# The first chunk's output product in seven half-size products, with the weights' sums scheduled sooner and their signs turned on ScalarE

## The chip, the cores and the metric

The kernel runs on one core of a Trainium2 chip. The metric is the device time of one execution in microseconds (us); the time before is the median of three runs. A profile of one execution gives the work of each engine: TensorE (PE, matmuls), VectorE (DVE), ScalarE (ACT), GpSimd (POOL), the DMA queues and the queue of SyncE (SP).

## The reference

For each of 4 batches, `q`, `k` and `v` are 6016 x 256. `q` and `k` are normalised over the 6016 rows of each column, a 256 x 256 matrix of scores is formed from them, and its softmax `a` is applied to `v`. The result, 24064 rows of 256, goes through a gated network: with `w_gate` and `w_val` of 256 x 1536 and `w_out` of 1536 x 256,

```
s = kn.transpose(0, 2, 1) @ qn / tau        # kn, qn: k, q over their column norms
a = softmax(s);  x = v @ a
out = (sigmoid(x @ w_gate) * (x @ w_val)) @ w_out
```

## The kernel before

**Folded weights.** Because `x = v @ a`, the kernel multiplies `a` into `w_gate` and `w_val` once for each batch (tiles `gh_G`, `gh_H`, function `gh`). The network then takes `v` itself, transposed into `vT`.

**Chunks and slots.** A batch is 47 tiles of 128 rows, in 12 chunks of up to 4 tiles (512 rows). A chunk has 12 *slots*, one for each 128 of the 1536 hidden columns. In a slot `glu` makes `ps_gate` (two matmuls of 512 columns, then a tanh on ScalarE, L662, into `g_sb`) and `ps_val` (two matmuls), and VectorE joins both into one slice of `hT` (L665). `ps_gate` and `ps_val` have two buffers each, so the gate of a slot needs the tanh of two slots before to be done. Slot numbers here run on over the chunks of a batch: slots 12 to 23 are those of the second chunk.

**The output product lies one chunk behind.** While chunk n runs through its 12 slots, the product of chunk n - 1's `hT` with `w_out` is done in twelve portions, one in each slot between gate and val (`run_work`, called through `mid`). Two forms of it exist:

- *plain* (`single`): for each of 4 row tiles, 12 matmuls of 256 columns that add up over the hidden columns; then one copy on ScalarE (L775). The first chunk of batch 0 alone is done so (`plain`).
- *seven products* (`product`): rows and columns are halved, and four half-size blocks are formed from seven products in place of eight, as in Strassen's scheme in Winograd's form. One round is for one pair of row tiles (p is 0 or 1), and each product is six matmuls of 128 columns. It needs sums and differences of blocks of `hT`, made on VectorE by `a_sum` (L691, L693, L695, tile `sums`, in two rounds for a chunk: `OWN_SLOTS` 7, 9, 11 of its own slots, `NEXT_SLOTS` 0, 2, 4 of the next chunk's), and of blocks of `w_out`, made once on GpSimd by `sum_w_out` (L232, tile `w_sums`, five sums in three pieces each). Sum 4 is also multiplied by -1 (L234). The order of the products is in `ORDER`: y1 of both pairs first (sum 1), then x1 (sum 0), z1 (sum 3), x2 and y2 (blocks of `w_out` itself), z2 (sum 2) and v2 (sum 4). `part` and `whole` put the seven results together: two copies on ScalarE for a pair, and four additions on GpSimd.

**The order of the work** is the order of the program: the scheduler is off (`manual_schedule`), each engine runs its own instructions in the order written, and waits only for what an instruction needs. `side_work` hangs further work on slots with `at(slot, function, ...)`; it is issued at the end of its slot. For batch 0: copying `w_out` to bf16 (`copy_w_out`, slot 8, L225), loads of the next batch's `q` and `k` (`load_qk`, L150) and of `v` (L162), the scores of the next batch (plain, from slot 14), the squares for its norms on ScalarE (L258), and the sums of `w_out` in slots 11, 13, 15, 17 and 19. The loads of `q`, `k`, `v` and of the weights are issued from GpSimd's queue; `w_out` is the last of the weights (L220, three pieces of 512 KB).

Of the kernel before, what the change touches and what calls it, by code (L numbers as in the profile page):

```python
# [12 lines left out]
ACT = mybir.ActivationFunctionType  # L13
ALU = mybir.AluOpType
# [37 lines left out]
OWN_SLOTS = {7: 0, 9: 1, 11: 2}  # L52
# [3 lines left out]
def kernel(  # L56
# [20 lines left out]
    nc = tc.nc  # L77
# [10 lines left out]
    FC = DFF // P  # L88
# [41 lines left out]
    def mm(out, lhsT, rhs, start, stop, **kw):  # L130
        nc.tensor.matmul(out, lhsT=lhsT, rhs=rhs, start=start, stop=stop, **kw)  # L131
# [34 lines left out]
    t0, nt = groups0[0]  # L166
# [39 lines left out]
    for f0, nf in pieces:  # L206
        if f0 + nf == DFF:
            load_v(0, 1)
        for w, src in enumerate((moe_w_gate, moe_w_val)):
            nc.gpsimd.dma_start(  # L210
                out=w_sb[w][f0 // FG][:, :, ds(f0 % FG, nf)],
                in_=src.rearrange("(t p) f -> p t f", p=P)[:, :, ds(f0, nf)],
# [5 lines left out]
    for n in range(FC // TPC):  # L218
        w_f32[n] = f32pool.tile([P, TPC, C], FP32, tag="f32", name="w_f32")
        nc.gpsimd.dma_start(  # L220
            out=w_f32[n], in_=moe_w_out.rearrange("(t p) c -> p t c", p=P)[:, n * TPC : (n + 1) * TPC, :]
# [5 lines left out]
    def sum_w_out(m, n):  # L227
        (k0, c0), op, (k1, c1) = B_SUMS[m]
        w = w_f32[n]
        out = w_sums[:, m, n * 2 : (n + 1) * 2, :]  # L230
        in0, in1 = w[:, k0::2, ds(c0 * P, P)], w[:, k1::2, ds(c1 * P, P)]
        nc.gpsimd.tensor_tensor(out=out, in0=in0, in1=in1, op=op)  # L232
        if m == 4:
            nc.gpsimd.tensor_scalar(out=out, in0=out, scalar1=-1.0, scalar2=None, op0=ALU.mult)  # L234


    st = {}
# [460 lines left out]
    stores = []  # L698

    def out_tile(b, ci):  # L700
        if (b, ci) not in ffn:
            ffn[b, ci] = opool.tile([P, TPC, C], FP32, tag="osb", name="out_sb")
        return ffn[b, ci]

    def out_work(b, ci):

        nt = groups[ci][1]
        half = nt // 2
        hT = hts[b, ci]
        work = []  # L710
        states = [{} for _ in range(half)]
        singles = {}
        plain = (b, ci) == (0, 0)

        def product(p, name, i):
            state = states[p]
            region, a, w = PRODUCTS[name]
            first = name == "y1" and i == 0
            if first:
                state["ps"] = pso.tile([P, CH], FP32, tag="o", name="ps_o")  # L720
            g, j = divmod(i, FC // 4)
            if isinstance(a, tuple):
                lhsT = hT[:, 2 * i + a[1], ds((a[0] * half + p) * P, P)]
            else:
                lhsT = sums[b, ci, g][:, a, j, ds(p * P, P)]
            rhs = w_out_sb[:, 2 * i + w[0], ds(w[1] * P, P)] if isinstance(w, tuple) else w_sums[:, w, i, :]
            mm(
                state["ps"][:, ds(region * P, P)],
                lhsT,
                rhs,  # L730
                start=first,
                stop=(i == FC // 2 - 1),
                skip_group_check=True,
            )
            if i == FC // 2 - 1:
                if name == "z1":
                    part(p)
                elif name == "v2":
                    whole(p)

        def part(p):

            m = states[p]["m"] = mpool.tile([P, 3, P], FP32, tag="m", name="m_sb")
            nc.scalar.copy(m, states[p]["ps"][:, : 3 * P].rearrange("p (n c) -> p n c", c=P))  # L744
            nc.gpsimd.tensor_tensor(out=m[:, 1, :], in0=m[:, 1, :], in1=m[:, 2, :], op=ALU.add)  # L745
            nc.gpsimd.tensor_tensor(out=m[:, 2, :], in0=m[:, 1, :], in1=m[:, 0, :], op=ALU.add)  # L746

        def whole(p):

            o = out_tile(b, ci)  # L750
            nc.scalar.copy(  # L751
                o[:, p : p + half + 1 : half, :],
                states[p]["ps"].rearrange("p (t c) -> p t c", c=C),
            )
            blocks = o.rearrange("p t (h c) -> p (t h) c", c=P)
            c00, c11 = 2 * p, 2 * (half + p) + 1
            ends = blocks[:, c00 : c11 + 1 : c11 - c00, :]
            mids = blocks[:, c00 + 1 : c11 : max(1, c11 - c00 - 2), :]
            last = (b, ci) == (B - 1, NCH - 2)
            add = nc.gpsimd.tensor_tensor  # L760
            add(out=ends, in0=ends, in1=states[p]["m"][:, 1:3, :], op=ALU.add)  # L761
            add(out=ends, in0=ends, in1=mids, op=ALU.subtract)  # L762
            if last:
                t0 = groups[ci][0]
                nc.sync.dma_start(out=out_rows[b][:, t0 + p : t0 + nt : half, :], in_=o[:, p:nt:half, :])
            elif p == half - 1:
                stores.append((b, ci))

        def single(s, f):
            if f == 0:  # L770
                singles[s] = pso.tile([P, CH], FP32, tag="o", name="ps_o")
            ps = singles[s]
            mm(ps[:, :C], hT[:, f, ds(s * P, P)], w_out_sb[:, f, :], f == 0, f == FC - 1)
            if f == FC - 1:
                nc.scalar.copy(out_tile(b, ci)[:, s, :], ps[:, :C])  # L775
                if plain and s == nt - 1:
                    stores.append((b, ci))

        if plain:
            return [(2, single, t, f) for t in range(nt) for f in range(FC)]  # L780
        for p, name in LAST_ORDER if (b, ci) == (B - 1, NCH - 2) else ORDER:
            if p < half:
                for i in range(FC // 2):
                    work.append((1, product, p, name, i))
                if nt % 2 and name == "z1":
                    for f in range(FC):
                        work.append((2, single, nt - 1, f))
        return work

    def run_work(work, share):  # L790

        upto = sum(w[0] for w in work) * share
        done = 0
        while work and done < upto:
            cost, fn, *args = work.pop(0)
            fn(*args)
            done += cost

    def store():
        while stores:  # L800
            b, ci = stores.pop(0)
            t0, nt = groups[ci]
            nc.sync.dma_start(out=out_rows[b][:, t0 : t0 + nt, :], in_=ffn.pop((b, ci))[:, :nt, :])
# [111 lines left out]
    def side_work(b):  # L915
# [4 lines left out]
        def at(slot, fn, *a):  # L920
            side.setdefault(divmod(slot, FC), []).append((fn, a))

        for ci in range(NCH):
            nb, nci = (b, ci + 1) if ci + 1 < NCH else (b + 1, 0)
            lb, lci = (b, ci + 2) if ci + 2 < NCH else (b + 1, ci + 2 - NCH)
            if nb < B:
                at(ci * FC + 2, transpose_v, nb, nci)
            if lb < B:
                at(ci * FC + (10 if (b, ci) == (0, 0) else 0), load_v, lb, lci)
            if (b, ci) == (0, 0):  # L930
                for i in range(FC // TPC):
                    at(8, copy_w_out, i)
                for n, m in enumerate((1, 0, 3, 2, 4)):
                    for i in range(FC // TPC):
                        at(11 + 2 * n, sum_w_out, m, i)
        n = b + 1
        if n == B:
            return side
# [3 lines left out]
        for g, (t0, nt) in enumerate(groups if b == 0 else []):  # L942
# [4 lines left out]
            for w in range(2):  # L947
                at(s0 + 1 + 4 * w, narrow_square, n, g, w)
                slot = s0 + 3 + 4 * w
# [51 lines left out]
        for i, piece in enumerate(gh_order):  # L1001
            slot = GH_SLOTS[i]
# [12 lines left out]
    def gh_pieces(ns):  # L1015
        for n in ns:
            gh(0, gh_first[n], *gh_banks[n % 4])

    prev = None
    for b in range(B):  # L1020
        side = side_work(b)
        for ci in range(NCH):
            final = (b, ci) == (B - 1, NCH - 1)
            for f in range(FC):
                mid = gh_mid.get(f) if (b, ci) == (0, 0) else None
                if prev is not None:
                    mid = lambda: run_work(work, 1 / max(1, FC - final - f))
                elif mid is not None:
                    mid = lambda ns=mid: gh_pieces(ns)
                glu(b, ci, f, mid)  # L1030
                if prev is not None:
                    if f == 4:
                        store()
                    next_sums = LAST_SLOTS if final else NEXT_SLOTS
                    if f in next_sums and prev != (0, 0):
                        a_sum(*prev, 1, next_sums[f])
                if f in OWN_SLOTS and not final and (b, ci) != (0, 0):
                    a_sum(b, ci, 0, OWN_SLOTS[f])
                for fn, a in spill.get((b, ci, f), []) + side.get((ci, f), []):
                    fn(*a)  # L1040
                if (b, ci) == (0, 0):
                    gh_pieces(gh_end.get(f, ()))
            prev = (b, ci)
            if not final:
                work = out_work(*prev)
# [39 lines left out]
```

## Time and profile before

| | |
|---|---|
| time, median of 3 | 800.55 us (800.33 to 804.13) |
| span of the profiled execution | 798.6 us |
| busy: TensorE, VectorE, ScalarE, GpSimd | 779.1, 680.8, 512.9, 409.0 us |
| sums of w_out on GpSimd (L232) | 15, first at 52.5 us, last at 65.7 us, median 728 ns |
| signs on GpSimd (L234) | 3, 848 to 1643 ns |
| first chunk's plain matmuls, 52 to 69 us | 48 of 128x256 |

The span counts from the profile's start. [...] consecutive matmuls overlap, and what one costs is read from the distance of their starts. In a list of instructions in order of time the columns are start, duration, engine, line, operation and tiles, how many were merged, and in brackets the idle time before and what ended it. All matmuls but the transposes have line L131, that of a helper.

### The profile page before, as it was taken

The numbers are of one execution on the slowest core, as the hardware profiler recorded it, in microseconds if no ns is written. First come the engines' busy times: TensorE is split into PE (matmuls) and PEld (weight loads), VectorE is DVE, ScalarE is ACT, GpSimd is POOL, SyncE is SP. The second block draws the span as 40 slices with busy tenths as digits, with TensorE's granted clock in tenths as the row PEclk, the third lists the DMA queues.
The fourth block names the chain that finished last, engine by engine and source line by source line (L and its number), as shares of the span: only waits on it lengthen the run. The fifth ranks groups of instructions, "written<-read, shape, count | busy, mean of one in ns | idle before, by whom it ended". The sixth has DMA issues, their size and how long they took to land.

```text
span 798.6 us, 18098 instructions
## 1 busy us (share of the span) xinstructions
PE 779.1 (98%) x6875; PEld 498.0 (62%) x6875; DVE 680.8 (85%) x1056; ACT 512.9 (64%) x891; POOL 409.0 (51%) x633
## 2 busy tenths in 40 slices
PE   3899999999999999999999999999999999999998
PEld 2556666666666666666666666666666666666666
DVE  5767898898889999998989999999898888888885
ACT  3766777765676767665667776766665565565553
POOL 3566445346453666555943566654754234334333
PEclk9999999999999999999999999999999999999999
DMA  9997859432685898752586599856234423423302
GB/s 214 204 196 121 143 97 142 88 67 54 135 143 102 151 181 150 135 101 53 103 148 121 104 177 163 152 113 108 54 67 85 69 54 81 80 54 79 75 27 73
DMA packets 85303, 89.12 MB, mean 112 GB/s; under 512 B 52704, under 2 KB 58464, under 8 KB 85216
## 3 DMA queue, kind: packets, MB, share of 16 engines
q0 software_dynamic: 28144, 49.82, 37.3%
q1 hardware_dynamic: 56496, 37.30, 21.4%
q8 instruction: 53, 0.87, 0.4%
q10 hardware_dynamic: 576, 0.85, 0.3%
q14 instruction: 34, 0.28, 0.1%
HBM read 79.04 MB, written 24.64 MB: 130 GB/s over the span
## 4 chain that ended last, share of the span: by engine, by line
PE 95%; DMA 4%; DVE 0%; issue 0%; ACT 0%; POOL 0%; DVEq 0%; POOLq 0%
PE ps_gate L131 31%; PE ps_val L131 31%; PE ps_o L131 28%; DMA qk_sb<-in_k_dram 4%; PE ps_s L131 4%; PE ps_gh L131 3%; PE ps_end L131 0%; PE ps_n L131 0%; DVE x_sb L525 0%; PE ps_r L131 0%; ACT e_sb L543 0%; POOL qk_sb L150 0%; DVE x_sb L537 0%; DVE r L508 0%; DVE end L825 0%
## 5 line engine op out<-in xcount | busy, mean ns | idle before, releaser
L662 ACT ACTIVATE g_sb<-ps_gate 128x512 f32<-128x512 f32 (+1 forms) x576 | 338.4, 588 | 248.0 <-PE ps_gate L131 236.0
L665 DVE SCALAR_TENSOR_TENSOR hT<-g_sb,ps_val 128x512 bf16<-128x512 f32 (+1 forms) x576 | 387.0, 672 | 98.4 <-PE ps_val L131 69.3
L131 PE MATMUL ps_gate<-vT,gh_G 128*128 128x512 bf16 (+1 forms) x1152 | 337.6, 375 | 0.0
L131 PE MATMUL ps_val<-vT,gh_H 128*128 128x512 bf16 (+1 forms) x1152 | 337.5, 375 | 0.0
L131 PEld LDWEIGHTS <-sums 128*128 128x128 bf16 x2670 | 183.0, 98 | 82.0
L761 POOL TENSOR_TENSOR out_sb<-out_sb,m_sb 128x256 f32<-128x256 f32 x89 | 69.1, 776 | 203.3 <-ACT out_sb L751 175.8
L131 PEld LDWEIGHTS <-gh_G 128*128 128x128 bf16 x1152 | 104.2, 98 | 82.2 <-DVE gh_G L611 0.3
L131 PE MATMUL ps_o<-w_sums,sums 128*128 128x128 bf16 x1602 | 154.0, 219 | 0.0
L131 PEld LDWEIGHTS <-hT 128*128 128x128 bf16 x1200 | 88.2, 98 | 46.6
L745 POOL TENSOR_TENSOR m_sb<-m_sb 128x128 f32<-128x128 f32 x89 | 48.0, 539 | 128.8 <-ACT m_sb L744 128.6
L762 POOL TENSOR_TENSOR out_sb<-out_sb 128x256 f32<-128x256 f32 x89 | 93.4, 1049 | 7.0
L131 PE MATMUL ps_o<-w_out_sb,sums 128*128 128x128 bf16 x1068 | 96.2, 219 | 0.0
L695 DVE TENSOR_TENSOR sums<-hT 128x1536 bf16<-128x1536 bf16 (+1 forms) x92 | 96.1, 1044 | 0.0
L131 PE MATMUL ps_o<-w_sums,hT 128*128 128x128 bf16 x1068 | 95.4, 219 | 0.0
L131 PEld LDWEIGHTS <-gh_H 128*128 128x128 bf16 x1152 | 90.1, 98 | 3.3 <-DVE gh_H L611 0.3
L693 DVE TENSOR_TENSOR sums<-hT 128x1536 bf16<-128x1536 bf16 (+1 forms) x92 | 86.1, 936 | 0.0
L131 PEld LDWEIGHTS <-qk_sb 128*128 128x128 bf16 x286 | 29.5, 103 | 43.1 <-issue 10.0
L751 ACT COPY out_sb<-ps_o 128x512 f32<-128x512 f32 x89 | 51.7, 580 | 0.0
L691 DVE TENSOR_TENSOR sums<-hT 128x768 bf16<-128x768 bf16 (+1 forms) x92 | 51.5, 559 | 0.0
L746 POOL TENSOR_TENSOR m_sb<-m_sb 128x128 f32<-128x128 f32 x89 | 46.4, 522 | 7.0
L131 PE MATMUL ps_s<-qk_sb 128*128 128x256 bf16 (+1 forms) x194 | 34.7, 297 | 15.2 <-DMA qk_sb<-in_k_dram 8.6
L258 ACT ACTIVATE sq<-qk_sb 128x1024 bf16<-128x1024 bf16 (+3 forms) x36 | 35.7, 1011 | 12.2 <-DMA qk_sb<-in_k_dram 12.0
(104 smaller groups left out, 551.0 us busy)
## 6 DMA issues: line engine op xcount, KB each, us to landing
out_dram<-out_sb SPq DMA_DIRECT2D x43, 512.0 KB, 3.4
v_sb<-in_v_dram POOLq DMA_DIRECT2D x44, 256.0 KB, 5.3
acc<-sq POOLq DMA_DIRECT2D x36, 256.0 KB, 5.0
qk_sb<-in_q_dram POOLq DMA_DIRECT2D x35, 256.0 KB, 7.3
qk_sb<-in_k_dram POOLq DMA_DIRECT2D x35, 256.0 KB, 6.5
qk_sb<-in_q_dram POOLq DMA_DIRECT2D x4, 512.0 KB, 11.4
qk_sb<-in_k_dram POOLq DMA_DIRECT2D x4, 512.0 KB, 13.3
w_f<-in_moe_w_out_dram POOLq DMA_DIRECT2D x3, 512.0 KB, 10.0
```

The source lines that it names most:

```text
L131: nc.tensor.matmul(out, lhsT=lhsT, rhs=rhs, start=start, stop=stop, **kw)
L258: nc.scalar.activation(out=sq[:, :nt, :], in_=src[:, :nt, :], func=ACT.Square)
L662: nc.scalar.activation(out=g_sb[:, :n], in_=ps_gate[:, :n], func=ACT.Tanh, scale=0.5)
L665: nc.vector.scalar_tensor_tensor(out=hts[b, ci][:, f, :n], in0=g_sb[:, :n], scalar=1.0, in1=ps_val[:, :n], op0=ALU.add, op1=ALU.mult,)
L691: nc.vector.tensor_tensor(out=out[:, :, 0], in0=x[:, :, 0, 0], in1=x[:, :, 1, 1], op=ALU.add)
L693: nc.vector.tensor_tensor(out=out, in0=x[:, :, 0], in1=x[:, :, 1], op=ALU.add)
L695: nc.vector.tensor_tensor(out=out, in0=x[:, :, :, 0], in1=x[:, :, :, 1], op=ALU.subtract)
L745: nc.gpsimd.tensor_tensor(out=m[:, 1, :], in0=m[:, 1, :], in1=m[:, 2, :], op=ALU.add)
L746: nc.gpsimd.tensor_tensor(out=m[:, 2, :], in0=m[:, 1, :], in1=m[:, 0, :], op=ALU.add)
L751: nc.scalar.copy(o[:, p : p + half + 1 : half, :], states[p]["ps"].rearrange("p (t c) -> p t c", c=C),)
L761: add(out=ends, in0=ends, in1=states[p]["m"][:, 1:3, :], op=ALU.add)
L762: add(out=ends, in0=ends, in1=mids, op=ALU.subtract)
```

## The change

The first chunk's output product takes the seven-product form too. `plain` goes, and with it the conditions that kept the first chunk's `a_sum` from being made. For this the sums of `w_out` are needed twelve slots sooner, at slot 12 in place of slot 24, and `sum_w_out` moves to slots 10, 11, 13, 14 and 16. The multiplication of sum 4 by -1 moves from GpSimd to ScalarE.

```diff
@@ sum_w_out
         if m == 4:
-            nc.gpsimd.tensor_scalar(out=out, in0=out, scalar1=-1.0, scalar2=None, op0=ALU.mult)
+            nc.scalar.activation(out=out, in_=out, func=ACT.Copy, scale=-1.0)
@@ out_work
-        plain = (b, ci) == (0, 0)
...
-        if plain:
-            return [(2, single, t, f) for t in range(nt) for f in range(FC)]
@@ side_work
                 for i in range(FC // TPC):
                     at(8, copy_w_out, i)
-                for n, m in enumerate((1, 0, 3, 2, 4)):
+                for slot, m in ((10, 1), (11, 0), (13, 3), (14, 2), (16, 4)):
                     for i in range(FC // TPC):
-                        at(11 + 2 * n, sum_w_out, m, i)
+                        at(slot, sum_w_out, m, i)
@@ the loop over batches, chunks and slots
-                    if f in next_sums and prev != (0, 0):
+                    if f in next_sums:
                         a_sum(*prev, 1, next_sums[f])
-                if f in OWN_SLOTS and not final and (b, ci) != (0, 0):
+                if f in OWN_SLOTS and not final:
                     a_sum(b, ci, 0, OWN_SLOTS[f])
```

The words "plain scores in the second batch" in the change's description name what the kernel before does as well: batch 1's scores are formed without the seven products.

More of the change, by code (lines that the diff above doesn't have):

```diff
@@ L775, in single @@
                 nc.scalar.copy(out_tile(b, ci)[:, s, :], ps[:, :C])
-                if plain and s == nt - 1:
-                    stores.append((b, ci))
-        if plain:
-            return [(2, single, t, f) for t in range(nt) for f in range(FC)]
         for p, name in LAST_ORDER if (b, ci) == (B - 1, NCH - 2) else ORDER:
```

## The prediction, made before the changed kernel ran

> **What bounds the kernel now.** I read the page first: busy times by engine, then the chain that ended last.
>
> ```profile
> PE 779.1 (98%) x6875; PEld 498.0 (62%) x6875; DVE 680.8 (85%) x1056; ACT 512.9 (64%) x891; POOL 409.0 (51%) x633
> PE 95%; DMA 4%; DVE 0%; issue 0%; ACT 0%; POOL 0%; DVEq 0%; POOLq 0%
> ```
>
> TensorE (PE) is the bound and the other engines look idle enough. But the change sits in one place, the first two chunks, so I then asked for the waits of TensorE after 34 us and for the busy time by stage.
>
> ```profile
> PE ps_r L131 <- ACT e_sb L543: 0.7, 1, 0.7
> ...
> 34.00:52.00 18.00, 17.32 (x101) 8.72 (x101) 13.79 (x26) 12.68 (x24) 9.61 (x15) 1.00 1.04 198
> 52.00:69.00 17.00, 17.00 (x111) 10.66 (x110) 9.76 (x15) 10.90 (x19) 16.70 (x25) 1.00 0.89 152
> 69.00:798.60 729.60, 726.14 (x6540) 465.80 (x6537) 635.53 (x975) 472.08 (x830) 368.26 (x566) 1.00 0.56 104
> ```
>
> The first line is all that TensorE waits for after 34 us: once. From there on it has no slack, so every microsecond it is made to wait is added to the end, and none is won back. In the columns PE, PEld, DVE, ACT, POOL, the stretch 52 to 69 us (slots 12 to 23, where the first chunk's output product runs) shows GpSimd (POOL) busy 16.70 of 17.00 us, against 51% over the span: the engine that makes the weights' sums is full just where the change asks it to be sooner. Last, the timelines of TensorE and of GpSimd there.
>
> ```profile
> 51.98 0.60 PE L131 MATMUL ps_o<-w_out_sb,hT 128*128 128x256 bf16 x4
> 52.42 0.59 PE L131 MATMUL ps_val<-vT,gh_H 128*128 128x512 bf16 x2
> ...
> 68.89 0.55 PE L131 MATMUL ps_o<-w_sums,hT 128*128 128x128 bf16 x7
> 69.28 0.59 PE L131 MATMUL ps_val<-vT,gh_H 128*128 128x512 bf16 x2
> ```
> ```profile
> 48.86 1.04 POOL L225 CAST w_out_sb<-w_f 128x1024 bf16<-128x1024 f32 x1 [0.53 <-DMA w_f<-in_moe_w_out_dram]
> 49.85 0.57 POOL L150 DMA_DIRECT2D qk_sb<-in_q_dram  x1
> ...
> 51.98 0.58 POOL L162 DMA_DIRECT2D v_sb<-in_v_dram  x1
> 52.53 2.14 POOL L232 TENSOR_TENSOR w_sums<-w_f 128x256 bf16<-128x256 f32 x3
> 54.58 0.57 POOL L162 DMA_DIRECT2D v_sb<-in_v_dram  x1
> 55.17 4.15 POOL L232 TENSOR_TENSOR w_sums<-w_f 128x256 bf16<-128x256 f32 x6
> ```
>
> Slot 12 reaches its output product at 51.98 us; the sums' first consumer comes only at 68.89. GpSimd cannot start the first sum before 52.53: it waits for the last third of w_out to land (48.86), casts it, and issues five loads of about 0.53 us. A sum takes 0.69 us of the queue (4.15 / 6).
>
> [...]
> 1. [...] four of 256 columns take 52.42 - 51.98 = 0.44 us, seven of 128 take 69.28 - 68.89 = 0.39.
> 2. [...]
> 3. [...]
>
> ```profile
> 102.91 1.32 POOL L762 TENSOR_TENSOR out_sb<-out_sb 128x256 f32<-128x256 f32 x1
> ```
> ```profile
> 102.28 1.37 DVE L695 TENSOR_TENSOR sums<-hT 128x1536 bf16<-128x1536 bf16 x1
> ```
> L695 otherwise takes 0.95, and L762 0.72 at its least: one block costs GpSimd 0.6 us.
>
> 4. [...] Here a gap of 3.05 us was enough:
>
> ```profile
> 20.39 3.20 PE L131 MATMUL ps_s<-qk_sb 128*128 128x256 bf16 x16 [3.05 <-DMA qk_sb<-in_k_dram]
> ...
> 25.27 1.91 PE L131 MATMUL ps_s<-qk_sb 128*128 128x256 bf16 x16 [0.44 <-DMA qk_sb<-in_k_dram]
> ```
> The same sixteen matmuls cost 1.3 us more. A longest gap of 2.12 us before it left the clock at 1.00 in that stretch.
>
> **The change, part by part.**
>
> *Fewer columns.* Twelve groups of four matmuls become twelve of seven: 12 x (0.44 - 0.39) = **-0.6 us**, all on the path.
>
> *First wait, slot 12: product y1 needs sum 1.* In the built order its third piece is the eighth GpSimd instruction after the last cast (five loads, three sums): 52.53 + 3 x 0.69 = 54.6 undisturbed. New on VectorE are six operand sums (L691, L693, L695: two rounds of 0.55 + 0.95 + 0.95 us) in slots 7 to 16, with two SBUF inputs each, and L695 of slot 11 falls at 53 to 54 us, on these three. Low bound no block, high bound two; I take one, 0.6: 55.2. Three matmuls later (0.17) the group ends at 55.4, against 52.42: lag **3.0**. The delay of VectorE by the same six (TensorE's ps_val in slot 10 would be held up to 0.8 us) is hidden inside this wait.
>
> *Second wait, slot 14: z1 needs sum 3.* GpSimd goes on: three pieces of sum 0 (2.07) to 57.3, a load of v (0.55) to 57.85, pieces of sum 3 at 58.55, 59.25, 59.95. TensorE, after ps_val, gate, a group, ps_val, gate (4 x 0.43 + 0.39) and four matmuls (0.22), is there at 55.4 + 2.3 = 57.75, and waits for the second piece, 59.25; the group ends at 59.3 against 55.02 before: lag **4.3**. x1's own wait for sum 0 (57.3) is met in passing.
>
> *Third wait, slot 19: the signs on ScalarE.* They leave GpSimd (3.4 us by three L234) and stand on ScalarE between the tanh of slot 16 and that of slot 17, each waiting for a piece of sum 4. GpSimd: sum 2 to 62.0, one block by L693 of slot 14 to 62.6; then the first chunk's two m_sb additions, new here, about 0.53 each (63.65); two loads (64.75); three pieces of sum 4: 66.85. The sign itself is not in the trace; the nearest rows, 128x256 out of PSUM, are 0.37 (L775, copy) and 0.47 (L609, with a scale): I take 0.4, last sign at 67.3. Then tanh of slot 17, 0.6: 67.9. Everything on ScalarE is queued behind the signs, the tanh of slot 17 first; ps_gate has two buffers, so the gate of slot 19 waits for the tanh of slot 17. TensorE would be at that gate at 61.31 + 4.3 - 4 x 0.05 = 65.4; it starts at 67.9: lag **6.6**. It starts at 61.31 in the trace before:
>
> ```profile
> 61.31 0.59 PE L131 MATMUL ps_gate<-vT,gh_G 128*128 128x512 bf16 x2
> ```
>
> *Slots 19 to 23* give back 5 x 0.05: lag 6.4. After that everything is as before, shifted.
>
> *At nothing:* the larger evictions (two m_sb of 0.47 and two out_sb of 0.58 for four L775 of 0.37) lie on ScalarE, which is busy 10.90 of 17.00 us here and catches up in the slots after 19; the first chunk's later GpSimd additions and the delayed loads for the next batch lie beside a GpSimd that waits for ScalarE (4.50 and 1.45 us idle at 74 to 77 us), and those loads are asked for a dozen slots ahead.
>
> Sum: 800.55 + 6.6 - 0.25 = 806.9, say **807.0 us**, 0.8% slower.
>
> **The rivals.**
> - *No blocks on GpSimd (15%).* Every piece 1.2 us sooner at the end of the chain: sum 4 at 65.65, gate 19 at 66.7, lag 5.4, end 5.2 later: 805.7. For it: in the trace L691 at 63.48 ran beside a GpSimd instruction almost unhindered (0.59 against 0.55). Against: 102.91 above.
> - *More blocks or the clock (22%).* Two blocks more add 1.2; gaps of about 2.5 us in slots 12 and 19 lie between 2.12, which kept the clock, and 3.05, which lost it; a loss costs 1.3: 808.2 to 809.5.
> - *ScalarE's wait is not felt (5%).* If ps_gate's buffers or an earlier sum 4 cover it, only lag 4.3 less 9 x 0.05 stays: 804.4, within 0.5%.
> - *The sums come in time (3%).* Were w_out to land some 4 us sooner and the sums' wait gone, only the 0.6 us remains: 799.95, not slower. The transfer's three landings (45.3 to 48.9 us) with DMA at 1.04 of its engines in that stretch speak against it.
> - *Faster by over 0.5% (2%)* would take 4 us, and the matmuls give 0.6: this is for what I have overlooked.
>
> **How the numbers follow.** My forecast has 53% and gives 807.0. Leaving out the two lowest rivals and the far end of the clock's, the range goes from 804.7 (no block, and the pieces of w_out landing 1 us sooner, the spread that I allow three landings in one trace) to 809.5. 0.5% is 4.0 us, 804.55: slower 0.53 + 0.15 + 0.22 = 0.90, same 0.05 + 0.03 = 0.08, faster 0.02.
>
> **What would show it.** In the trace of after: TensorE waits on GpSimd's w_sums around 53 to 55 us and again near 58 to 59; ScalarE waits on GpSimd near 64 to 67 with 128x256 signs; the gate of slot 19 waits for ScalarE about 2.5 us; total waits of TensorE after 34 us rise from 0.7 to about 7.5; L232 pieces lengthened to 1.3 where a VectorE sum runs. I am wrong if the first sum starts well before 52.5, if TensorE's third wait is missing, or if the clock of the stretch 52 to 75 falls under 1.00.

## The result, and the profile after

The changed kernel takes **807.92 us** (median of six, 807.03 to 809.99) against 800.55 us: ratio 1.0089, 95% interval 1.0067 to 1.0112. It is 0.9% slower. The forecast was 807.0 us, slower, in a range of 804.7 to 809.5.

The page of the changed kernel, busy time (TensorE 783.7 us against 779.1) and chain, looks much like that of before: TensorE is still the engine that the end hangs on. What is new is 4% of the chain on GpSimd, where there was none.

```profile
PE 91%; DMA 4%; POOL 4%; issue 0%; ACT 0%; DVE 0%; POOLq 0%; ACTq 0%
```

TensorE's waits after 34 us say where it goes (total us, times, longest). Before, the wait of ps_r stood alone with 0.7 us; now three others of slots 10 to 19 stand beside it, each behind another engine (besides one of 0.4 us right at 34 us).

```profile
PE ps_gate L131 <- ACT g_sb L662: 2.5, 1, 2.5
PE ps_o L131 <- POOL w_sums L232: 2.1, 3, 1.1
PE ps_val L131 <- DVE hT L665: 0.7, 1, 0.7
```

TensorE's timeline places them. The wait of ps_val falls in slot 10, the three for sum 1's pieces in slot 12, and the gate's in slot 19.

```profile
51.71 0.59 PE L131 MATMUL ps_val<-vT,gh_H 128*128 128x512 bf16 x2 [0.69 <-DVE hT L665]
...
54.14 0.27 PE L131 MATMUL ps_o<-w_sums,hT 128*128 128x128 bf16 x2 [0.54 <-POOL w_sums L232]
54.82 0.27 PE L131 MATMUL ps_o<-w_sums,hT 128*128 128x128 bf16 x2 [0.41 <-POOL w_sums L232]
56.22 0.33 PE L131 MATMUL ps_o<-w_sums,hT 128*128 128x128 bf16 x3 [1.12 <-POOL w_sums L232]
...
69.32 0.59 PE L131 MATMUL ps_gate<-vT,gh_G 128*128 128x512 bf16 x2 [2.49 <-ACT g_sb L662]
```

Behind the two long waits lies a second kind of loss. In the busy times by stretch of the changed kernel the third number from the end is the granted clock. It is 0.54 and 0.51 in two stretches of 3.6 and 3.5 us soon after these waits, and 1.00 in the stretches between.

```profile
56.40:60.00 3.60, 3.60 (x18) 1.83 (x16) 1.74 (x3) 0.60 (x1) 3.58 (x6) 0.54 1.00 162
...
70.30:73.80 3.50, 3.50 (x17) 1.89 (x15) 1.71 (x3) 2.34 (x4) 0.72 (x2) 0.51 0.02 5
```

The two stretches lose 3.6 x 0.46 + 3.5 x 0.49 = 3.4 us. The gate of slot 24 starts at 77.92 us, 9.46 later than before; the span is 9.4 longer (808.0 against 798.6). So nothing that happens after slot 24 matters, and nothing is won back. Of the 9.46, 5.25 are the idle times shown. 0.8 more belongs to the same five waits: idle time is counted from the end of the last matmul's listed duration, which lies 0.16 us behind the moment at which the next could have started (two matmuls of 512 columns are listed with 0.59 us and start 0.43 us ahead of what follows). 3.4 are the clock, 0.6 a later head (slot 10's gate starts at 50.42 in place of 49.82), less 0.6 for fewer columns. (This sums what lies on TensorE's path; it is not what the kernel would win without one of the parts.) The profiled execution has one of the longer spans of the six: granted clocks over the span were 0.993 to 0.997, and the spans followed them (808.0 and 808.2 at 0.993, 805.3 to 806.3 at 0.995 to 0.997). By these clocks, how often it falls differs from run to run; the other executions have no trace that would show it.

GpSimd and ScalarE show what stands behind the waits. On GpSimd (start, duration) six sums take 4.97 and 4.86 us, where undisturbed ones took 4.15: three of the fifteen lasted 1.36 to 1.44 us in place of 0.71, each beside one of VectorE's operand sums (L695 at 54.62 us, L693 at 61.87, L695 at 64.89).

```profile
53.25 4.97 POOL L232 TENSOR_TENSOR w_sums<-w_f 128x256 bf16<-128x256 f32 x6
...
58.76 4.86 POOL L232 TENSOR_TENSOR w_sums<-w_f 128x256 bf16<-128x256 f32 x6
...
65.61 2.72 POOL L232 TENSOR_TENSOR w_sums<-w_f 128x256 bf16<-128x256 f32 x3
```

On ScalarE the signs stand where the forecast put them. The first waits 2.74 us for sum 4, and the tanh behind the third releases the gate of slot 19.

```profile
67.00 0.42 ACT L234 ACTIVATE w_sums<-w_sums 128x256 bf16<-128x256 bf16 x1 [2.74 <-POOL w_sums L232]
...
68.37 0.42 ACT L234 ACTIVATE w_sums<-w_sums 128x256 bf16<-128x256 bf16 x1 [0.27 <-POOL w_sums L232]
68.69 0.58 ACT L662 ACTIVATE g_sb<-ps_gate 128x512 f32<-128x512 f32 x1
```

### The profile page after: what moved, and what is told of

Its sections match the earlier page's. It is cut to its first block, busy times and chain, and to the rows that moved or that the text cites. A ratio compares the mean times of both kernels' runs of the same rounds, so it can differ in the third digit from the quotient of the medians.

```text
span 808.0 us, 18172 instructions
## 1 busy us (share of the span) xinstructions
PE 783.7 (97%) x6897; PEld 500.1 (62%) x6911; DVE 687.3 (85%) x1062; ACT 514.2 (64%) x894; POOL 411.8 (51%) x638
## 3 DMA queue, kind: packets, MB, share of 16 engines
q0 software_dynamic: 28144, 49.82, 36.9%
## 4 chain that ended last, share of the span: by engine, by line
PE 91%; DMA 4%; POOL 4%; issue 0%; ACT 0%; DVE 0%; POOLq 0%; ACTq 0%
PE ps_gate L131 29%; PE ps_val L131 29%; PE ps_o L131 27%; PE ps_s L131 4%; DMA qk_sb<-in_k_dram 3%; PE ps_gh L131 2%; POOL w_sums L232 2%; DMA w_f<-in_moe_w_out_dram 1%; POOL qk_sb L150 1%; POOL w_gate L210 0%; POOL w_val L210 0%; POOL v_sb L162 0%; POOL w_out_sb L225 0%; PE ps_end L131 0%; ACT g_sb L662 0%
## 5 line engine op out<-in xcount | busy, mean ns | idle before, releaser
L131 PEld LDWEIGHTS <-sums 128*128 128x128 bf16 x2730 | 187.4, 98 | 84.3 <-issue 0.6
L131 PE MATMUL ps_o<-w_sums,sums 128*128 128x128 bf16 x1638 | 158.0, 220 | 0.0
L131 PEld LDWEIGHTS <-hT 128*128 128x128 bf16 x1176 | 85.7, 98 | 47.5 <-issue 2.4
L131 PE MATMUL ps_o<-w_sums,hT 128*128 128x128 bf16 x1092 | 98.4, 220 | 2.1 <-POOL w_sums L232 2.1
L761 POOL TENSOR_TENSOR out_sb<-out_sb 128x256 f32<-128x256 f32 x91 | 95.4, 1049 | 7.1
L131 PE MATMUL ps_o<-w_out_sb,sums 128*128 128x128 bf16 x1092 | 98.7, 220 | 0.0
L695 DVE TENSOR_TENSOR sums<-hT 128x1536 bf16<-128x1536 bf16 (+1 forms) x94 | 98.5, 1048 | 0.0
L693 DVE TENSOR_TENSOR sums<-hT 128x1536 bf16<-128x1536 bf16 (+1 forms) x94 | 88.6, 942 | 0.0
L691 DVE TENSOR_TENSOR sums<-hT 128x768 bf16<-128x768 bf16 (+1 forms) x94 | 53.5, 569 | 0.0
L131 PE MATMUL ps_s<-qk_sb 128*128 128x256 bf16 (+1 forms) x194 | 36.4, 310 | 13.8 <-DMA qk_sb<-in_k_dram 6.9
```

The source lines that it names most:

```text
L691: nc.vector.tensor_tensor(out=out[:, :, 0], in0=x[:, :, 0, 0], in1=x[:, :, 1, 1], op=ALU.add)
L693: nc.vector.tensor_tensor(out=out, in0=x[:, :, 0], in1=x[:, :, 1], op=ALU.add)
L695: nc.vector.tensor_tensor(out=out, in0=x[:, :, :, 0], in1=x[:, :, :, 1], op=ALU.subtract)
```

## The experiments

Theory: the loss is waits of TensorE, in the first half for sums 1 and 3 and in slot 19 for ScalarE, plus the clock that falls after a wait; the seven products themselves cost nothing. Rivals: the form of the product costs time itself, or the sign on ScalarE costs as work and not by its place in the queue. Each is a change of the changed kernel unless another is named; "over before" is measured against the kernel before on the same chip (800.58 to 800.67 us).

### E1: the signs back on GpSimd

```diff
-            nc.scalar.activation(out=out, in_=out, func=ACT.Copy, scale=-1.0)
+            nc.gpsimd.tensor_scalar(out=out, in0=out, scalar1=-1.0, scalar2=None, op0=ALU.mult)
```

> The changed kernel with the signs of sum 4 back on GpSimd. My theory (three waits on GpSimd's queue, the third handed on through ScalarE): the gate of slot 19 no longer waits for ScalarE (2.5 us in the changed kernel), but product v2 now waits for the longer GpSimd queue, about 1.5 to 2 us in slot 20, so 805.5 to 807.5. Rival (the signs' place on ScalarE is itself the cost): the whole wait and the half-clock stretch after it go, about 804.

Measured: 808.05 us, ratio 1.0090 (1.0075 to 1.0105), a little above what was expected. The gate's wait is gone, but the signs lengthen GpSimd's queue, and product v2 waits for them instead; a wait for an operand sum of VectorE is new as well:

```profile
PE ps_o L131 <- POOL w_sums L232: 2.1, 3, 1.1
PE ps_o L131 <- POOL w_sums L234: 1.9, 2, 1.6
PE ps_o L131 <- DVE sums L691: 0.9, 1, 0.9
```

The clock averaged 0.67 in 56 to 60 us and 0.57 in 72 to 76. Undoing this part alone gains nothing; the place of the signs is not what the first half's waits come from.

### E2: the plain product, with the sums in their new slots and the signs on ScalarE

```diff
+        plain = (b, ci) == (0, 0)
...
+        if plain:
+            return [(2, single, t, f) for t in range(nt) for f in range(FC)]
...
-                    if f in next_sums:
+                    if f in next_sums and prev != (0, 0):
...
-                if f in OWN_SLOTS and not final:
+                if f in OWN_SLOTS and not final and (b, ci) != (0, 0):
```

> The kernel before with its plain product for the first chunk, but with the weights' sums in the new slots and the signs on ScalarE: nothing needs the sums before slot 24. My theory: the signs block ScalarE's queue all the same, until sum 4 is there (64.6 us), tanh of slot 17 ends at 65.6 and the gate of slot 19 starts 4.3 us late; with a half-clock stretch after so long a gap, 804.9 to 806.6. Rival (only the product's own need of the sums costs): 800.6.

Measured: 807.18 us, ratio 1.0080 (1.0065 to 1.0095). No product needs a sum before slot 24 here, and still nearly the whole loss is there. Beside ps_r's, one wait is left, and the clock after it is 0.52 and 0.63 in two stretches of 4 us:

```profile
PE ps_gate L131 <- ACT g_sb L662: 3.7, 1, 3.7
```
```profile
64.00:68.00 4.00, 2.69 (x9) 1.28 (x9) 1.38 (x2) 3.31 (x7) 1.90 (x4) 0.52 1.29 163
68.00:72.00 4.00, 4.00 (x20) 2.18 (x18) 1.84 (x3) 1.23 (x3) 0.00 (x0) 0.63 1.01 186
```

The wait was expected; that it would cost two half-clock stretches was not, and so the time is above the expected one.

### E3: the seven products with blocks of w_out in place of the sums

The first chunk's products read `w_out_sb` where they would read `w_sums`, so the first chunk's output is another one; the sums and the signs keep the slots and the engine that they had before.

```diff
...
+            if (b, ci) == (0, 0) and not isinstance(w, tuple):
+                w = (w % 2, w // 2 % 2)
...
```

> Seven products for the first chunk with blocks of w_out itself in place of the weights' sums (so the first chunk's output is another one), the sums and signs as in the kernel before. No wait for sums is left, all else of the seven-product form is there: fewer columns, six operand sums on VectorE, other evictions. My theory: -0.6 for the columns, up to 0.7 for the one wait on VectorE in slot 10: 799.9 to 800.9. Rival (the form itself is dear here): over 802.

Measured: 801.11 us (800.05 to 802.04, twelve runs), ratio 1.0005 (0.9996 to 1.0013), a little above the expected 799.9 to 800.9. The only wait of TensorE after 34 us is ps_r's 0.7. The rival that the form itself costs is out: seven products with all their operand sums, larger evictions and additions cost nothing that can be measured (the interval leaves room for 1.0 us). The 0.6 us of fewer columns doesn't show in the median either; the profiled execution has a span of 798.3 us against 798.6.

### E4: sum 4, with its sign, in one VectorE instruction

```diff
         if m == 4:
-            nc.scalar.activation(out=out, in_=out, func=ACT.Copy, scale=-1.0)
+            nc.vector.scalar_tensor_tensor(out=out, in0=in0, scalar=-1.0, in1=in1, op0=ALU.mult, op1=ALU.subtract)
+        else:
+            nc.gpsimd.tensor_tensor(out=out, in0=in0, in1=in1, op=op)
```

> The changed kernel with sum 4 and its sign made in one instruction on VectorE, at the same slot. My theory: the third wait (2.5 us) and the half-clock stretch after it (1.7) go, the waits of slots 12 and 14 stay: 803.2 to 805. Rival (ScalarE's wait only takes the place of one that GpSimd's late sums force anyway): 806.5 or more.

Measured: 804.98 us, ratio 1.0051 (1.0036 to 1.0066), as expected: 2.9 us less than the changed kernel. The third wait is gone and the first stays, piece for piece as in the changed kernel (0.54, 0.42 and 1.12 us in slot 12). But the clock was 1.00 from 34 us on, and now slot 14's wait can be seen:

```profile
58.84 0.27 PE L131 MATMUL ps_o<-w_sums,sums 128*128 128x128 bf16 x2 [0.67 <-POOL w_sums L235]
59.52 0.22 PE L131 MATMUL ps_o<-w_sums,sums 128*128 128x128 bf16 x1 [0.40 <-POOL w_sums L235]
```

It is the second wait of the prediction, which the changed kernel's trace doesn't have. There the half clock of 56.4 to 60 us slows TensorE by more than this wait (1.7 us against 1.07), so that the sum is in time.

### E5: sum 1 ahead of the casts

```diff
+                    at(8, sum_w_out, 1, i)
+                for i in range(FC // TPC):
                     at(8, copy_w_out, i)
-                for slot, m in ((10, 1), (11, 0), (13, 3), (14, 2), (16, 4)):
+                for slot, m in ((11, 0), (13, 3), (14, 2), (16, 4)):
```

> The changed kernel with the three pieces of sum 1 ahead of the casts of w_out on GpSimd, each made as its third of w_out lands. My theory (what counts is how much GpSimd has queued before sums 3 and 4, not the order within it): the wait of slot 12 goes, but sum 0 now comes after the casts and loads, at about 56 us, and slot 13 waits for it; slots 14 and 19 wait as before, so 806.5 to 808.5. Rival (the wait of slot 12 is the loss): about 804.

Measured: 808.44 us, ratio 1.0094 (1.0080 to 1.0107), as expected. Slot 12 no longer waits for a sum; slot 13 waits 2.29 us for the next one. What counts in the first half is the total of GpSimd's queue up to each sum, not which sum goes first.

### E6: everything moved

In the list of slots, `None` stands for the casts. Sum 1 goes ahead of the casts and loads, sums 0 and 3 come before the casts, the products run y, x, z, v for one pair after the other (`LAST_ORDER`), the operand sums move to slots 12 to 17, and sum 4 is made on VectorE as in E4.

```diff
-                for slot, m in ((10, 1), (11, 0), (13, 3), (14, 2), (16, 4)):
+                for slot, m in ((8, 1), (10, 0), (12, 3), (13, None), (14, 2), (15, 4)):
...
+                    if prev == (0, 0):
+                        if f < 6:
+                            a_sum(0, 0, f % 2, f // 2)
```

> All of it put right: sum 1 ahead of the loads and casts, then the loads, sums 0 and 3, the casts, sum 2; sum 4 with its sign in one instruction on VectorE in slot 15; the first chunk's products in the order that has x1 of the second pair ahead of z1; its six operand sums on VectorE in slots 12 to 17 and none before. My theory: no wait of TensorE is left and only the fewer columns show: 799.9 to 800.4 where the kernel before gives 800.6. Rival (VectorE, with six sums in six slots, becomes the bound there): 801.5 or more.

Measured: 807.69 us, ratio 1.0084 (1.0071 to 1.0097). Far off the expected 799.9 to 800.4; its rival, VectorE as the bound, gave 801.5 or more. TensorE's one new wait was 4.5 us, and for VectorE, not for GpSimd; behind it the clock was 0.50 in 60 to 64 us. The next fences show VectorE's and then GpSimd's timeline: L692 is an operand sum that takes 0.55 us elsewhere.

```profile
53.86 2.42 DVE L692 TENSOR_TENSOR sums<-hT 128x768 bf16<-128x768 bf16 x1
56.20 0.67 DVE L666 SCALAR_TENSOR_TENSOR hT<-g_sb,ps_val 128x512 bf16<-128x512 f32 x1
56.80 4.32 DVE L692 TENSOR_TENSOR sums<-hT 128x768 bf16<-128x768 bf16 x1
```
```profile
51.66 4.18 POOL L235 TENSOR_TENSOR w_sums<-w_f 128x256 bf16<-128x256 f32 x6
55.75 0.58 POOL L162 DMA_DIRECT2D v_sb<-in_v_dram  x1
56.32 3.02 POOL L225 CAST w_out_sb<-w_f 128x1024 bf16<-128x1024 f32 x3
59.29 2.40 POOL L235 TENSOR_TENSOR w_sums<-w_f 128x256 bf16<-128x256 f32 x3
```

The first L692 ends at 56.28, about 0.5 us after GpSimd's sums end and a load is issued (55.75); the second begins as three casts follow and ends at 61.12, during the last sums. VectorE was held up not by one GpSimd instruction (a cast takes 1.05 us there, a sum 0.7) but by a row of them, and what stands behind it on VectorE came later too: the next hT starts at 61.04 us.

### E7: the changed kernel with its waits filled

Matmuls of 512 columns whose result nothing reads are put into the waits: nine in slot 12 and nine ahead of slot 19.

```diff
...
+                at(18, busy_m, 9)
...
+                if prev == (0, 0):
+                    for where, n in ((4, 5), (2, 2), (0, 2)):
+                        work.insert(where, (0, busy_m, n))
```

> The changed kernel with 18 matmuls that nobody reads put into TensorE's waits of slots 12 (nine) and 19 (nine), to keep its clock up. My theory: no half-clock stretch between 50 and 76 us; the wait of slot 14, which the slow clock hid, shows again with 1 to 1.5 us, so 806.0 to 807.2, with less spread between runs. Rival (the clock doesn't depend on these gaps): 808 or more, from the matmuls added.

Measured: 807.19 us, ratio 1.0079 (1.0063 to 1.0095), as expected. The clock is 1.00 in every stretch from 34 us to slot 24 and on, and slot 14 waits for sum 3 (0.66 and 0.40 us), as in E4. So by the medians the clock is worth only some 0.7 us, and the spread of the runs (807.03 to 809.99 against 806.58 to 807.64) does not set even that clear of nothing. Its first fall covers a wait that comes back without it, and by the granted clocks not every run has both falls.

### E8: E2 with slot 19's wait filled

```diff
+                at(18, busy_m, 16)
```

> The plain product with the sums' new slots and the signs on ScalarE, and 16 matmuls that nobody reads in TensorE's wait of slot 19. My theory: the wait itself costs 4.2 us and the clock 2.5 to 3.4 us of the 6.6 that this kernel loses without the filling; with the clock kept, 804.3 to 805.2. Rival (the clock is not lost through the gap): 807 or more.

Measured: 805.19 us, ratio 1.0052 (1.0038 to 1.0067), clock 1.00, as expected. By the medians, of E2's 6.5 us over before the clock is 2.0 (807.18 - 805.19) and the wait the other 4.5. The split is rough: in E2's profiled execution the gate of slot 19 starts 3.9 us later than it could, and the slowed matmuls take 2.8 us more.

### E9: E6 with casts on ScalarE and the operand sums set around GpSimd's sums

Sum 2 also moves to slot 16, and the pieces of sum 4 to slots 13 and 16.

```diff
-        nc.gpsimd.tensor_copy(out=w_out_sb[:, n * TPC : (n + 1) * TPC, :], in_=w_f32[n])
+        nc.scalar.copy(w_out_sb[:, n * TPC : (n + 1) * TPC, :], w_f32[n])
...
+                for slot, i in ((13, 0), (16, 1), (16, 2)):
+                    at(slot, sum_w_out, 4, i)
+                for slot, g, m in ((8, 0, 0), (12, 1, 0), (14, 0, 1), (15, 1, 1), (17, 0, 2), (18, 1, 2)):
+                    at(slot, a_sum, 0, 0, g, m)
```

> The kernel with all moved, its GpSimd queue opened where VectorE has sums to make: the casts of w_out on ScalarE (slots 12, 13, 14), sum 2 behind the first pair's additions (slot 16), the operand sums of the first chunk in slots 8, 12, 14, 15, 17, 18, sum 4 with its sign on VectorE a piece or two at a time (slots 13 and 16). Theory now (VectorE's operand sums are locked out as long as GpSimd has instructions back to back): no wait of TensorE on VectorE's sums over 0.5 us, no half-clock stretch, 799.9 to 800.9. Rival (VectorE is simply overloaded by the six sums): a wait of 2 us or more stays, over 802.5.

Measured: 805.41 us, ratio 1.0059 (1.0046 to 1.0072); expected was 5 us less, and the rival's sign (VectorE overloaded: a wait of 2 us or more, over 802.5 us) was met. One operand sum still took 2.41 us (at 54.58, beside six GpSimd sums), and then VectorE had no idle time to catch up in: it is busy 4.00 of 4.00 us in 56 to 60 and in 60 to 64, and TensorE waits 2.9 us for the last operand sums.

### E10: E6 with the casts alone moved to ScalarE

```diff
-        nc.gpsimd.tensor_copy(out=w_out_sb[:, n * TPC : (n + 1) * TPC, :], in_=w_f32[n])
+        nc.scalar.copy(w_out_sb[:, n * TPC : (n + 1) * TPC, :], w_f32[n])
```

> The kernel with all moved, and one edit: the three casts of w_out on ScalarE in slots 12, 13 and 14 in place of GpSimd. GpSimd's second row of back-to-back work is then three sums (about 2.1 us) in place of three casts and three sums. Lock-out theory: the second operand sum L692 takes about 2 us in place of 4.3, TensorE's wait for it falls from 4.5 to 1.5 to 2.5 us, and the time to 801.8 to 804.5. Rival (VectorE overloaded): unchanged at 807 or more.

Measured: 804.43 us, ratio 1.0047 (1.0032 to 1.0063), 3.3 us less than E6 and within the expected time. With no casts to follow the sums, the second operand sum is back at its own length, where 2 us were expected:

```profile
53.95 3.02 DVE L692 TENSOR_TENSOR sums<-hT 128x768 bf16<-128x768 bf16 x1
...
57.48 0.55 DVE L692 TENSOR_TENSOR sums<-hT 128x768 bf16<-128x768 bf16 x1
```

The first is held up as before, and VectorE is again without idle time from 56 to 64 us. TensorE waits 3.2 us for operand sums, more than the expected 1.5 to 2.5. So in E9 and E10 both things are seen, operand sums held up beside GpSimd's work and a VectorE with no time left, and these runs don't part them.

### E11: E2 with the signs in slot 22

```diff
+                for i in range(FC // TPC):
+                    at(22, sign_w_out, i)
```

> The plain product with the sums' new slots and the signs on ScalarE, but the signs put into slot 22, when sum 4 has long been made. Theory (a strict queue: the signs cost through waiting ahead of the tanh of slot 17, not through their 0.4 us each): 800.4 to 801.0, as the kernel before. Rival (ScalarE can't take the extra work): 803 or more.

Measured: 800.57 us (twelve runs), ratio 0.9999 (0.9991 to 1.0008), as expected. The same three signs stand on ScalarE, find sum 4 done, and cost nothing:

```profile
67.00 1.02 ACT L236 ACTIVATE w_sums<-w_sums 128x256 bf16<-128x256 bf16 x3
```

E2 and E11 differ in the slot of three instructions and, each over before, by 6.5 us. The rival that ScalarE's added work costs is out.

### E12: the sums spread among the loads

Sum 1 first, casts on ScalarE in slots 12 to 14, GpSimd's other sums spread between loads, signs on ScalarE in slots 19 and 20, and the products in the order y, x, z and the rest.

```diff
-                for slot, m in ((10, 1), (11, 0), (13, 3), (14, 2), (16, 4)):
-                    for i in range(FC // TPC):
+                for slot, m, pieces_n in (
+                    (8, 1, (0, 1, 2)), (10, 0, (0, 1)), (11, 0, (2,)), (11, 3, (0,)), (12, 3, (1, 2)),
+                    (13, 2, (0, 1)), (14, 2, (2,)), (14, 4, (0,)), (16, 4, (1, 2)),
+                ):
+                    for i in pieces_n:
...
+                for slot, i in ((19, 0), (20, 1), (20, 2)):
+                    at(slot, sign_w_out, i)
...
-                at(max(FC - 3, s0 - 12), load_qk, n, t0, nt)
+                at({0: 9, 1: 10, 2: 13}.get(g, s0 - 12), load_qk, n, t0, nt)
```

> The changed kernel with its plan for the first chunk changed: sum 1 is formed first, the three casts of weights go to ScalarE (slots 12 to 14), GpSimd's other sums are spread between its loads so that no more than two or three stand back to back, the two signs are turned on ScalarE late (slots 19 and 20), the operand sums of the first half stand in slots 7, 9 and 11 and those of the second in 12, 14 and 16, and the products run x, y and z first, v last. Theory (what the changed kernel loses is waits for weights' sums, their clock stretches, and VectorE locked out by long runs of GpSimd sums, none of which belongs to the seven products themselves): no wait of TensorE over 0.5 us for a sum, clock 1.00 in every stretch after 34 us, 799.9 to 801.0 us. Rival (GpSimd and VectorE cannot carry the first chunk's sums beside their other work in any order): a wait of 2 us or more for a sum remains and the time is over 802.5.

In this kernel the third matmul of the first pair's v2, in slot 20, reads its piece of sum 4 before the sign is turned, so a part of the first chunk's output is another one. Measured: a median of 804.83 us (801.37 to 807.01, six runs), ratio 1.0054 (1.0041 to 1.0067): above the expected 799.9 to 801.0. The profiled execution is the fastest of the six, 801.37 us, and shows nearly what was expected: clock 1.00 in every stretch, no wait for any sum, and one new wait, in slot 12, for VectorE's hT:

```profile
PE ps_o L135 <- DVE hT L671: 0.8, 1, 0.8
```

VectorE is busy 4.00 of 4.00 us in 48 to 52 and in 52 to 56 there, and two operand sums take 1.84 and 2.28 us (0.95 undisturbed). The five other executions have no trace; their spans are 802.3 to 805.2 us with clocks of 0.995 to 0.998. The rival's time came true without its mechanism being seen. That the sums can come without a wait is shown by this one execution, of a kernel whose output is another one; what spoils it in the others stays open.

## Why the prediction was right, and where it was off

The forecast held in direction, in mechanism and nearly in size (0.9 us low). The steps can be read from where the gate of a slot starts, against before and less the head (the lag of slot 10: 0.60 in the changed kernel, 0.31 in E7):

| gate of slot | predicted lag | changed kernel | E7, clock 1.00 |
|---|---|---|---|
| 13 (after the first wait) | 3.0 | 3.50 | 2.74 |
| 15 (after the second) | 4.3 | 4.95 | 4.03 |
| 19 (after the third) | 6.6 | 7.41 | 6.15 |
| 24 | 6.35 | 8.86 | 5.92 |

- *First wait:* right. Its pieces add up to 2.07 us, and 0.69 stand ahead of it in slot 10. This was the VectorE delay that the prediction put at up to 0.8 us and costed at nothing because the first wait would hide it. It is hidden: the first wait ends when sum 1 is done, whenever TensorE arrives, and E7's lag of 2.74 is not above 3.0.
- *Second wait:* right in size where the clock stays up (E4: 1.07, E7: 1.06; predicted 4.3 - 3.0 = 1.3). In the profiled execution of the changed kernel it doesn't appear, because the half clock took its place. For the same reason TensorE's waits after 34 us add up to 6.2 us there and not to the forecast's 7.5.
- *Third wait:* right. Gate 19 waits 2.49 us for the tanh behind the signs (predicted 2.5), a sign takes 0.416 us (taken at 0.4), and E11 shows that it is place and not work. That the tanh of slot 17 waits behind the signs was taken for granted in the prediction; the trace of before has no wait of ScalarE on GpSimd that would show it. E2 against E11 shows it: 6.5 us from the queue position of three instructions.
- *Fewer columns, and the edits at nothing:* right within what can be measured. E3 has the evictions, additions and operand sums of the new form and comes to 801.11 us.
- *Blocks on GpSimd:* a block is an instruction there that lasts longer beside an operand sum of VectorE; its 0.6 us was an estimate from one pair in the trace of before. One was taken up to sum 1 and one more up to the signs; the trace has three of about 0.7 us in all. The third lengthens sum 4 (its first piece takes 1.36 us at 65.61). GpSimd has no idle time from its loads at 50.6 us to the end of sum 4, so the block moves the gate of slot 19: 7.41 in place of 6.6. In E7 it is missing (sum 4 takes 2.10 us in place of 2.72), and the gate's lag is 6.15.
- *The other term that was mis-sized is the clock.* It was left to a rival, at 1.3 us a loss and with 22%. In the profiled execution it fell twice, at 1.7 us each. The first fall did not reach the end, since TensorE had to wait in slot 19 in any case, for a sum and signs that GpSimd and ScalarE make at their own pace. (By another way it may have: in E7, L695 ends at 64.64 us, just before sum 4 begins at 64.69, so a small shift of TensorE's work could have put the third block there. That is not shown.) The second did: from slot 19 to slot 24 the lag grows by 1.45 where 0.25 was to be won back. So of the 2.5 us between 6.35 and 8.86, 0.8 are the block and 1.7 the second fall. In the median run less of it is there: E7, without it, is only 0.7 us faster, within the spread of the runs.
- *The ground for the clock's price was misread.* The gap of 2.12 us was taken as one that kept the clock, because the clock column gives 1.00 there. But the sixteen matmuls behind it took 3.56 us, those behind the next gap 1.91: TensorE was slow there whatever the column says. Behind the gap of 3.05 us the column does show it, 0.50 in 20.81 to 24.22 us of the kernel before. In the changed kernel's trace sixteen matmuls behind a gap of 2.09 us (at 25.35) took 3.04 us, most of it at a clock of 0.50. So gaps of 2.5 us were likelier to lose the clock than the prediction had it.

The rival of more blocks or the clock came as close as the forecast: the median, 807.92, lies between 807.0 and that rival's 808.2, nearer to the latter, and both of its parts were seen. That the forecast is only 0.9 us low is in part luck. The rival's mechanism ran together with the forecast's rather than in its place. The prediction's condition for being wrong, a clock under 1.00 in 52 to 75 us, was met, and the sum was still close, since a fall of the clock and a later wait overlap.

The rival of no blocks (805.7) and that of an unfelt ScalarE wait (804.4) are against the trace. The rival of sums in time, 799.95, needed what only E3 and E12's fastest execution come near, and E3 shows that its reward is under what can be measured.

## What to carry to other kernels

Before an instruction moves to a less busy engine, write down what it waits for and what stands behind it in that queue: three instructions of 0.4 us cost 6.5 us in one slot and nothing six slots later. Where a new consumer asks for a result twelve slots sooner, add up the producer's queue to that result, loads and casts with it; its mean load over the span (51% here) says nothing of a stretch in which it is full. And ask first what the change could bring if all went well: here 0.6 us, so that no wait at all was affordable.

## What the runs showed of the hardware

- **The same waits can keep or lose the clock, by where they lie.** In slot 12 the changed kernel waited 0.54, 0.41 and 1.12 us in pieces and then ran 3.4 us at half clock; E4 waited 0.54, 0.42 and 1.12 us and stayed at 1.00. Read from the clock in stretches of 0.25 us, the changed kernel's falls begin at 25.95, 56.66 and 70.32 us and last 3.41 us each, and between their starts lie 9 and 4 times 3.41. Stretches of 3.41 us, counted back and on from one of a trace's own falls, show the difference. The first fence is the changed kernel, the second E4; in a line the stretch is followed by its length and by TensorE's busy time in it:

```profile
53.26:56.67 3.41, 1.33 (x11) 0.69 (x10) 2.33 (x4) 0.70 (x2) 3.41 (x5) 1.00 1.11 208
```
```profile
51.14:54.55 3.41, 2.29 (x12) 0.98 (x11) 3.41 (x5) 1.24 (x3) 3.41 (x6) 1.00 1.07 174
54.55:57.97 3.42, 2.46 (x22) 1.51 (x22) 1.92 (x4) 0.60 (x1) 3.42 (x5) 1.00 1.11 206
```
  The waits fill one stretch of the changed kernel (2.08 us idle) and are shared by two of E4 (1.12 and 0.96). Cut so, from 17 us on, the fourteen traces give one picture: each stretch at 1.00 that a fall followed had TensorE idle for 1.91 us or more (E1), and no stretch idle for 1.70 us or less (E6) was followed by one. No stretch lies between, so where the limit is stays open. E2's single gap of 3.74 us was followed by 6.8 us at half clock, two such stretches. On the changed kernel's lines one such stretch begins at 53.26 us, on E4's at 51.14 and 54.55; were these places to differ between runs of one kernel as well, so could the falls, but the runs without a trace can't show it.
- **A slowed stretch ahead of a later wait can cost nothing.** In the profiled execution the first fall's 1.7 us was covered by the waits behind it; only the second's 1.7 reached the end.
- **A VectorE instruction can be held up over a row of GpSimd instructions.** In E6 a 0.55 us operand sum took 4.32 us, across two casts and at least one sum that began after it; in E10, with the casts on ScalarE, it took 0.55, and the operand sum before it, beside six GpSimd sums, 3.02. In the changed kernel L695, at 54.62 beside six sums, took 0.97 us, and it was GpSimd that lost 0.7. Which of the two happens I could not tell from these runs.
